# Softmax row sums folded once per four slots instead of once per two, values four slots behind, output copies on ScalarE

## The chip, the cores and the metric

The kernel runs on one core of one Trainium2 chip. The metric is device time in microseconds (us). Executions of one kernel agree within about 0.3%, periods between start times inside the traces to about 0.01 us.

## The reference, cut to what matters

There are two independent attention blocks, A and B, of 16 batches, 32 query positions, 32 query heads over 4 key/value heads, 512 keys and head size 128, all in bf16.

```python
q = (x @ wq).reshape(B, Sq, Hq, Dh).transpose(0, 2, 1, 3)
k = repeat(k_cache, 8, axis=1);  v = repeat(v_cache, 8, axis=1)
scores = einsum("bhqd,bhkd->bhqk", q, k) * Dh ** -0.5
o = einsum("bhqk,bhkd->bhqd", softmax(scores), v)
out = o.transpose(0, 2, 1, 3).reshape(B, Sq, Hq * Dh) @ wo     # A and B side by side
```

## The kernel before

The main loop has 128 **slots**; a slot is one batch and one key/value head (8 query heads, 256 query columns). In each slot TensorE computes transposed scores into `s_ps` (four matmuls of 256 columns), ScalarE takes the exponential into `p_sb`, VectorE reduces `p_sb` over query position blocks into `parts`, and TensorE multiplies an *earlier* slot's `p_sb` with the values into `ob`, a bank of PSUM (the memory that this program's matmuls write) (four matmuls of 256 columns). Between them, `run(units, n)` issues matmuls of 512 columns from a **stream** of unrelated work: query projections first, output projections (`f_ps`) in the later part. So TensorE has something to do while the softmax chain runs. The **lag** is the number of slots by which the values matmuls run behind the scores: three in this kernel.

The row sums are spread over the partitions. `parts` becomes `cs` ("chunk sums") on VectorE; a small matmul, the **fold**, adds the four quadrants of partitions (the program types `cs` and the fold's matrix float32r; the trace shows them as f32 or fp32r); then VectorE takes the reciprocals, spreads them over columns with a transpose (`r`), and multiplies `ob` with `r` into `oT` ("normalize"). There is only one `ob` bank, and it holds a pair of slots.

```python
def fold_sums(j):                            # j: pair of slots
    cs = pair[j]
    sums = pair[j] = psum.tile([P, 2 * REP], FP32, name="sums", tag="sums", bufs=1)
    nc.tensor.matmul(sums[:], lhsT=fold[:]..., rhs=cs[:]..., start=True, stop=True)

def reciprocals(j):
    nc.vector.reciprocal(out=rall[:, j, :], in_=pair.pop(j)[:])
    r = rcp[j] = work.tile([P, 2 * REP, SQ], FP32, name="r")
    nc.vector.transpose(out=r[:]..., in_=rall[:, j, :].unsqueeze(2).to_broadcast(...))

# at the end of each output tile of the stream (f_units):
    if eng is nc.scalar: nc.scalar.copy(out=o_sb[:, 0:width], in_=ps[:, 0:width])
    else:                nc.vector.tensor_copy(out=o_sb[:, 0:width], in_=ps[:, 0:width])

for i in range(total_slots + 3):
    live = i < total_slots
    j, odd = divmod(i, 2)
    if live:
        do_loads(i); scores(i)
    run(units, 1)
    if not odd and 1 <= j <= NG: chunk_sums(j - 1)
    if i >= 3:                   values(i - 3)
    if odd and 1 <= j <= NG:     reciprocals(j - 1)
    if not odd and j >= 2:       normalize(j - 2)
    run(units, 5)
    if not odd and 1 <= j <= NG: fold_sums(j - 1)
    if live:                     partial_sums(i)
    run(units, 1 - (i % 4 == 3))
```

Of the kernel before, what the change touches and what calls it, by code (L numbers as in the profile page):

```python
# [8 lines left out]
BF16 = mybir.dt.bfloat16  # L9
FP32 = mybir.dt.float32  # L10
FP32R = mybir.dt.float32r
# [5 lines left out]
P = 128  # L17
# [3 lines left out]
REP = HQ // HKV  # L21
# [152 lines left out]
def kernel(  # L174
# [14 lines left out]
    nc = tc.nc  # L189
    B, SQ, D = A_x.shape  # L190
# [3 lines left out]
    KC = SK // P  # L194
    TT = NTOK // P
    NOUT = D
    NW = 512
    NH = NOUT // NW
    GRP = 4
    NG = B * HKV  # L200
    BPT = P // SQ
    QW = REP * SQ
# [7 lines left out]
    def fast_path(ok_i):  # L210
        with ExitStack() as fctx:
            enter = fctx.enter_context
            const = enter(tc.tile_pool(name="const", bufs=1))
            blk = enter(tc.tile_pool(name="blk", bufs=20))
            kv = enter(tc.tile_pool(name="kv", bufs=3))
            work = enter(tc.tile_pool(name="work", bufs=2))
            outp = enter(tc.tile_pool(name="outp", bufs=3))
            psum = enter(tc.tile_pool(name="psum", bufs=2, space=bass.MemoryType.PSUM))
            enter(tc.manual_schedule())

# [5 lines left out]
            nc.scalar.preload_act_table_set("natural_log_exp_and_others")  # L226


            warm = const.tile([P, NW], BF16, name="warm")
            nc.vector.memset(warm[:], 0.0)  # L230
            ident = const.tile([P, P], BF16, name="ident")
            make_identity(nc, ident[:])
# [1 line left out]
            for r in range(P // QD):  # L234
                rs = slice(r * QD, (r + 1) * QD)
                nc.vector.tensor_copy(
                    out=fold[rs],
                    in_=ident[rs, rs].unsqueeze(1).to_broadcast([QD, P // QD, QD]),
# [4 lines left out]
            nc.vector.memset(shift[:], SHIFT)  # L243
            cnt = const.tile([P, 1], FP32, name="cnt")
            nc.vector.memset(cnt[:], 0.0)
            rall = const.tile([P, NG, 2 * REP], FP32, name="rall")


            def blk_tile(shape, name, dtype=BF16):
# [76 lines left out]
            def f_units(pr, tt, n0, width, eng):  # L326
                ps = psum.tile([P, NW], FP32, name="f_ps", tag="proj")
                nh, off = divmod(n0, NW)
                for h in range(HQ):
                    assert all((pr, b, h // REP) in normalized for b in range(tt * BPT, (tt + 1) * BPT))  # L330
                    nc.tensor.matmul(  # L331
                        ps[:, 0:width],
                        lhsT=oT[pr, tt][:, h, :],
                        rhs=wo_tiles[pr, nh, h // REP][:, h % REP, off:off + width],
                        start=(h == 0),
                        stop=(h == HQ - 1),
                    )
                    if h == HQ - 1:
                        o_sb = outp.tile([P, NW], BF16, name="o_sb")
                        if eng is nc.scalar:  # L340
                            nc.scalar.copy(out=o_sb[:, 0:width], in_=ps[:, 0:width])  # L341
                        else:
                            nc.vector.tensor_copy(out=o_sb[:, 0:width], in_=ps[:, 0:width])  # L343
                        c0 = problems[pr][5] + n0
                        eng.dma_start(  # L345
                            out=out_flat[tt * P:(tt + 1) * P, c0:c0 + width],
                            in_=o_sb[:, 0:width],
                        )
                    yield
# [16 lines left out]
            def scores(i):  # L366
                pr, b, g = where(i)
                kT = k_tiles[i // GRP].rearrange("p q (k c) -> p q c k", c=KC)
                s_ps = psum.tile([P, KC, QW], FP32, name="s_ps", tag="s")
                for c in range(KC):  # L370
                    nc.tensor.matmul(  # L371
                        s_ps[:, c, :],
                        lhsT=kT[:, i % GRP, c, :],
                        rhs=qT[pr, g][:, b, :, :].rearrange("p h s -> p (h s)"),
                        start=True,
                        stop=True,
                    )
                p_sb = work.tile([P, KC, QW], BF16, name="p_sb", bufs=5)
                nc.scalar.activation(  # L379
                    out=p_sb[:], in_=s_ps[:], func=ACTF.Exp, bias=shift[:], scale=SCALE  # L380
                )
                st[i] = {"p": p_sb}

            parts, rcp, pair = {}, {}, {}

            def partial_sums(i):
                j, q = divmod(i, 2)
                if q == 0:
                    parts[j] = work.tile([P, 2, KC, REP], FP32, name="parts")
                nc.vector.tensor_reduce(  # L390
                    out=parts[j][:, q, :, :].rearrange("p c h -> p (c h)"),
                    in_=st[i]["p"][:].rearrange("p c (h s) -> p (c h) s", s=SQ),
                    axis=AX.X, op=ALU.add, apply_transpose=True,
                )

            def chunk_sums(j):
                cs = pair[j] = work.tile([P, 2, REP], FP32R, name="cs")
                with nc.allow_low_precision(reason="float32r holds the float32 sum"):
                    nc.vector.tensor_reduce(  # L399
                        out=cs[:], in_=parts.pop(j)[:].rearrange("p q c h -> p q h c"),  # L400
                        axis=AX.X, op=ALU.add,
                    )

            def fold_sums(j):
                cs = pair[j]
                sums = pair[j] = psum.tile([P, 2 * REP], FP32, name="sums", tag="sums", bufs=1)
                nc.tensor.matmul(  # L407
                    sums[:],
                    lhsT=fold[:].rearrange("p r s -> p (r s)"),
                    rhs=cs[:].rearrange("p q h -> p (q h)"),  # L410
                    start=True,
                    stop=True,
                )

            def reciprocals(j):
                nc.vector.reciprocal(out=rall[:, j, :], in_=pair.pop(j)[:])  # L416
                r = rcp[j] = work.tile([P, 2 * REP, SQ], FP32, name="r")
                nc.vector.transpose(  # L418
                    out=r[:].rearrange("p n s -> p (n s)"),
                    in_=rall[:, j, :].unsqueeze(2).to_broadcast([P, 2 * REP, SQ]),  # L420
                )

            ob = {}
# [1 line left out]
            def values(i):  # L425
                v_sb = v_tiles[i // GRP]
                j, q = divmod(i, 2)
                if q == 0:
                    ob[j] = psum.tile([P, 2, QW], FP32, name="ob", tag="ob", bufs=1)
                for c in range(KC):  # L430
                    nc.tensor.matmul(  # L431
                        ob[j][:, q, :],
                        lhsT=v_sb[:, i % GRP, c, :],
                        rhs=st[i]["p"][:, c, :],
                        start=(c == 0),
                        stop=(c == KC - 1),
                    )

            def normalize(j):
                for i in (2 * j, 2 * j + 1):  # L440
                    normalized.add(where(i))
                    st.pop(i)
                pr, b, g = where(2 * j)
                tt, bl = divmod(b, BPT)
                if (pr, tt) not in oT:
                    oT[pr, tt] = blk_tile([P, HQ, P], "oT")
                if pr == 0:
                    out = oT[pr, tt][:, g * REP:(g + 1) * REP, bl * SQ:(bl + 2) * SQ]
                    out = out.rearrange("p h (q s) -> p q h s", s=SQ)
                else:  # L450
                    out = oT[pr, tt][:, g * REP:(g + 2) * REP, bl * SQ:(bl + 1) * SQ]
                    out = out.rearrange("p (q h) s -> p q h s", h=REP)
                nc.vector.tensor_tensor(  # L453
                    out=out,
                    in0=rcp.pop(j)[:].rearrange("p (q h) s -> p q h s", h=REP),
                    in1=ob.pop(j)[:].rearrange("p q (h s) -> p q h s", s=SQ),
                    op=ALU.mult,
                )
# [79 lines left out]
            for h, copy in enumerate((nc.vector.tensor_copy, nc.scalar.copy)):  # L538
                copy(
                    out=qT[0, 0][:, :, h, :],  # L540
# [48 lines left out]


            total_slots = 2 * NG
            for i in range(total_slots + 3):
                live = i < total_slots
                j, odd = divmod(i, 2)
                if live:
                    do_loads(i)
                    scores(i)
                run(units, 1)
                if not odd and 1 <= j <= NG:
                    chunk_sums(j - 1)  # L600
                if i >= 3:
                    values(i - 3)
                if odd and 1 <= j <= NG:
                    reciprocals(j - 1)
                if not odd and j >= 2:
                    normalize(j - 2)
                run(units, 5)
                if not odd and 1 <= j <= NG:
                    fold_sums(j - 1)
                if live:  # L610
                    partial_sums(i)
                run(units, 1 - (i % 4 == 3))
# [56 lines left out]
```

## Time and profile before

The time is 350.51 us (median of 4 runs, 349.77 to 350.71); the profiled span is 348.6 us. These are the engine line of the page and some of its groups. PE is TensorE, PEld its weight loads, DVE VectorE, ACT ScalarE and POOL GpSimd; L407 is line 407 of the kernel. In a group line, the numbers after the first bar are total busy us and the mean ns of one instruction; those after the second are the engine's idle us just before them and what ended it.

```profile
PE 342.2 (98%) x2217; PEld 221.2 (63%) x2217; DVE 282.6 (81%) x420; ACT 180.4 (52%) x197; POOL 8.9 (3%) x21
...
L407 PE MATMUL sums<-cs,fold 128*128 128x16 f32 x64 | 22.9, 357 | 0.1
L407 PEld LDWEIGHTS sums<-cs,fold 128*128 128x128 f32 x64 | 12.1, 190 | 8.3 <-DVE cs L399 0.9
L343 DVE CAST o_sb<-f_ps 128x512 bf16<-128x512 f32 (+1 forms) x16 | 10.8, 673 | 10.8 <-PE f_ps L331 10.0
L399 DVE TENSOR_REDUCE cs<-parts 128x16 fp32r<-128x64 f32 x64 | 16.8, 262 | 2.2
L416 DVE RECIPROCAL rall<-sums 128x16 f32<-128x16 f32 x64 | 14.1, 220 | 0.0
```

TensorE is full. The first trap is the line of the folds: 64 of 357 ns look like 22.9 us, but matmuls are pipelined and their ends are modelled, so a mean duration is not what an instruction costs the stream. What it costs must be read from the **starts** of its neighbours. This is the timeline of PE (start us, us, engine, line, operation):

```profile
203.45 1.46 PE L331 MATMUL f_ps<-wo_sb,oT 128*128 128x512 bf16 x6
204.74 0.60 PE L371 MATMUL s_ps<-qT,kT 128*128 128x256 bf16 x4
...
205.83 1.24 PE L331 MATMUL f_ps<-wo_sb,oT 128*128 128x512 bf16 x5
206.72 0.36 PE L407 MATMUL sums<-cs,fold 128*128 128x16 f32 x1
206.94 0.39 PE L331 MATMUL f_ps<-wo_sb,oT 128*128 128x512 bf16 x1
207.17 0.60 PE L371 MATMUL s_ps<-qT,kT 128*128 128x256 bf16 x4
...
209.34 0.60 PE L371 MATMUL s_ps<-qT,kT 128*128 128x256 bf16 x4
...
210.43 1.24 PE L331 MATMUL f_ps<-wo_sb,oT 128*128 128x512 bf16 x5
211.74 0.28 PE L407 MATMUL sums<-cs,fold 128*128 128x16 f32 x1
...
212.10 0.60 PE L371 MATMUL s_ps<-qT,kT 128*128 128x256 bf16 x4
```

Six stream matmuls alone take 204.74 - 203.45 = 1.29 us; six with a fold among them take 207.17 - 205.83 = 1.34 us. So a fold costs about 0.05 us as this view rounds, not 0.357. The score lines work as a clock: from one `s_ps` line to the next is one slot, 2.43 us with a fold (204.74 to 207.17), and 2.385 or 2.17 us for slots of 7 or 6 stream matmuls without, which puts a fold at about 0.045 us. A group of four slots takes 9.407 us, and this repeats through the run.

The slot from 209.34 lasts 2.76 us, 0.33 us too long: the fold starts at 211.74 instead of about 211.3. VectorE's timeline for that stretch shows why:

```profile
209.54 0.69 DVE L343 CAST o_sb<-f_ps 128x512 bf16<-128x512 f32 x1 [0.77 <-PE f_ps L331]
210.15 1.23 DVE L390 TRANSPOSE_TENSOR_REDUCE parts<-p_sb 128x32 f32<-128x1024 bf16 x1
211.41 0.27 DVE L399 TENSOR_REDUCE cs<-parts 128x16 fp32r<-128x64 f32 x1
```

VectorE waited 0.77 us for the stream's output tile, copied it for 0.69 us, and only then came to the partial sums and the chunk sums that the fold needs. There is one other such hole, of about 0.12 us, in the slot from 299.14 us. Together the holes are 0.45 us.

### The profile page before, as it was taken

Reading aid. Unit: us, or ns where it says so; the run is one execution under the profiler, and the core shown is the slowest. Engines: PE = TensorE matmul, PEld = TensorE weight load, DVE = VectorE, ACT = ScalarE, POOL = GpSimd, SP = SyncE. Lnnn points to the kernel's source line nnn. Section 1 sums busy time; section 2 is a strip of 40 time slices with the busy share of each in tenths; the row PEclk is TensorE's granted clock in tenths of the full one; section 3 lists DMA queues with packets and bytes.
Section 4 is the critical chain, followed back from the end, with each engine's and each line's share of the span. In section 5 each row is a group of like instructions: output and inputs, shape, how many; then the busy total and the mean of one; then the engine's idle time right before and its main releaser. Section 6 shows DMA issues by size and latency. Waiting matters only on the chain.

```text
span 348.6 us, 5527 instructions
## 1 busy us (share of the span) xinstructions
PE 342.2 (98%) x2217; PEld 221.2 (63%) x2217; DVE 282.6 (81%) x420; ACT 180.4 (52%) x197; POOL 8.9 (3%) x21
## 2 busy tenths in 40 slices
PE   7999999999999999999999999999999999999995
PEld 4556666666666666666666666666666666666554
DVE  2118988888988889898889989999999999899710
ACT  3347667666666766666654454454455445445000
POOL 0000000000000000000000000000000000000010
PEclk9999999999999999999999999999999999999999
DMA  7999999899997899999999459995589995400000
GB/s 224 240 302 333 168 253 270 241 276 256 270 253 197 172 249 222 311 267 268 279 316 222 115 124 270 349 212 121 137 259 263 252 227 102 120 18 0 15 32 20
DMA packets 125069, 71.70 MB, mean 206 GB/s; under 512 B 73616, under 2 KB 124048, under 8 KB 125040
## 3 DMA queue, kind: packets, MB, share of 16 engines
q1 hardware_dynamic: 124176, 69.29, 81.7%
q0 software_dynamic: 720, 1.97, 1.7%
q8 instruction: 18, 0.29, 0.3%
q14 instruction: 11, 0.09, 0.1%
q10 hardware_dynamic: 144, 0.07, 0.1%
HBM read 51.38 MB, written 2.10 MB: 153 GB/s over the span
## 4 chain that ended last, share of the span: by engine, by line
PE 96%; DMA 2%; SPq 1%; DVE 1%; issue 0%; ACT 0%
PE f_ps L331 32%; PE q_ps L312 31%; PE ob L431 16%; PE s_ps L371 16%; DMA x_sb<-in_A_x_dram 2%; PE q_ps L516 1%; SPq L468 0%; DVE parts L390 0%; PE sums L407 0%; SPq L471 0%; DVE o_sb L343 0%; PE xT_ps L506 0%; ACT o_sb L341 0%; DVE cs L399 0%; PE ok_ps L627 0%
## 5 line engine op out<-in xcount | busy, mean ns | idle before, releaser
L379 ACT ACTIVATE p_sb<-s_ps,shift 128x1024 bf16<-128x1024 f32 x128 | 142.5, 1113 | 113.1 <-PE s_ps L371 100.4
L390 DVE TRANSPOSE_TENSOR_REDUCE parts<-p_sb 128x32 f32<-128x1024 bf16 x128 | 158.2, 1236 | 22.1 <-ACT p_sb L379 21.6
L331 PE MATMUL f_ps<-wo_sb,oT 128*128 128x512 bf16 (+1 forms) x544 | 133.3, 367 | 0.0
L312 PE MATMUL q_ps<-xT,wq_sb 128*128 128x512 bf16 x496 | 129.6, 380 | 0.0
L371 PE MATMUL s_ps<-qT,kT 128*128 128x256 bf16 x512 | 76.8, 273 | 0.0
L431 PE MATMUL ob<-p_sb,v_sb 128*128 128x256 bf16 x512 | 76.8, 273 | 0.0
L331 PEld LDWEIGHTS <-oT 128*128 128x128 bf16 x544 | 53.0, 98 | 33.8
L312 PEld LDWEIGHTS <-wq_sb 128*128 128x128 bf16 x496 | 48.4, 98 | 34.7 <-DMA wq_sb<-in_A_wq_dram 0.3
L371 PEld LDWEIGHTS <-kT 128*128 128x128 bf16 x512 | 56.9, 113 | 20.9
L431 PEld LDWEIGHTS <-v_sb 128*128 128x128 bf16 x512 | 50.1, 98 | 19.8 <-DVE oT L453 0.2
L453 DVE TENSOR_TENSOR oT<-r,ob 128x512 bf16<-128x512 f32 x64 | 43.9, 685 | 12.8 <-PE ob L431 9.4
L418 DVE STREAM_TRANSPOSE r<-rall 128x512 f32<-128x512 f32 x64 | 45.5, 711 | 2.2
L320 ACT CAST qT<-q_ps 128x512 bf16<-128x512 f32 x62 | 36.1, 583 | 21.3 <-PE q_ps L312 19.2
L407 PE MATMUL sums<-cs,fold 128*128 128x16 f32 x64 | 22.9, 357 | 0.1
L343 DVE CAST o_sb<-f_ps 128x512 bf16<-128x512 f32 (+1 forms) x16 | 10.8, 673 | 10.8 <-PE f_ps L331 10.0
L399 DVE TENSOR_REDUCE cs<-parts 128x16 fp32r<-128x64 f32 x64 | 16.8, 262 | 2.2
L407 PEld LDWEIGHTS sums<-cs,fold 128*128 128x128 f32 x64 | 12.1, 190 | 8.3 <-DVE cs L399 0.9
L345 POOL DMA_DIRECT2D out_dram<-o_sb x15 | 8.2, 549 | 329.3 <-DVE o_sb L343 298.6
L416 DVE RECIPROCAL rall<-sums 128x16 f32<-128x16 f32 x64 | 14.1, 220 | 0.0
L341 ACT CAST o_sb<-f_ps 128x256 bf16<-128x256 f32 x1 | 0.4, 372 | 22.1 <-PE f_ps L331 22.1
L509 DVE COPY xT<-xT_ps 128x512 bf16<-128x512 bf16 x4 | 1.7, 424 | 5.6 <-PE xT_ps L506 5.6
L509 ACT COPY xT<-xT_ps 128x512 bf16<-128x512 bf16 x4 | 2.3, 585 | 5.7 <-PE xT_ps L506 5.7
(27 smaller groups left out, 24.1 us busy)
## 6 DMA issues: line engine op xcount, KB each, us to landing
v_sb<-in_A_v_cache_dram SPq DMA_DIRECT2D x16, 512.0 KB, 5.0
wq_sb<-in_B_wq_dram SPq DMA_DIRECT2D x8, 1024.0 KB, 6.5
wo_sb<-in_A_wo_dram SPq DMA_DIRECT2D x8, 1024.0 KB, 7.6
v_sb<-in_B_v_cache_dram SPq DMA_DIRECT2D x16, 512.0 KB, 4.5
wo_sb<-in_B_wo_dram SPq DMA_DIRECT2D x8, 1024.0 KB, 8.8
wq_sb<-in_A_wq_dram SPq DMA_DIRECT2D x7, 1024.0 KB, 7.4
out_dram<-o_sb POOLq DMA_DIRECT2D x15, 128.0 KB, 3.6
x_sb<-in_A_x_dram SPq DMA_DIRECT2D x4, 256.0 KB, 3.9
```

What stands on the lines that cost most here:

```text
L312: nc.tensor.matmul(ps[:], lhsT=w[:, dc, (h % 4) * DH:(h % 4 + 1) * DH], rhs=xT[pr][:, dc, :], start=(dc == 0), stop=(dc == DC - 1),)
L320: nc.scalar.copy(out=qT[pr, g][:, :, hl, :], in_=ps[:].rearrange("p (b s) -> p b s", s=SQ),)
L331: nc.tensor.matmul(ps[:, 0:width], lhsT=oT[pr, tt][:, h, :], rhs=wo_tiles[pr, nh, h // REP][:, h % REP, off:off + width], start=(h == 0), ...
L371: nc.tensor.matmul(s_ps[:, c, :], lhsT=kT[:, i % GRP, c, :], rhs=qT[pr, g][:, b, :, :].rearrange("p h s -> p (h s)"), start=True, stop=True,)
L379: nc.scalar.activation(out=p_sb[:], in_=s_ps[:], func=ACTF.Exp, bias=shift[:], scale=SCALE)
L390: nc.vector.tensor_reduce(out=parts[j][:, q, :, :].rearrange("p c h -> p (c h)"), in_=st[i]["p"][:].rearrange("p c (h s) -> p (c h) s", s=SQ),
L399: nc.vector.tensor_reduce(out=cs[:], in_=parts.pop(j)[:].rearrange("p q c h -> p q h c"), axis=AX.X, op=ALU.add,)
L407: nc.tensor.matmul(sums[:], lhsT=fold[:].rearrange("p r s -> p (r s)"), rhs=cs[:].rearrange("p q h -> p (q h)"), start=True, stop=True,)
L416: nc.vector.reciprocal(out=rall[:, j, :], in_=pair.pop(j)[:])
L418: nc.vector.transpose(out=r[:].rearrange("p n s -> p (n s)"), in_=rall[:, j, :].unsqueeze(2).to_broadcast([P, 2 * REP, SQ]),)
L431: nc.tensor.matmul(ob[j][:, q, :], lhsT=v_sb[:, i % GRP, c, :], rhs=st[i]["p"][:, c, :], start=(c == 0), stop=(c == KC - 1),)
L453: nc.vector.tensor_tensor(out=out, in0=rcp.pop(j)[:].rearrange("p (q h) s -> p q h s", h=REP), in1=ob.pop(j)[:].rearrange("p q (h s) -> p ...
```

## The change

`k` now counts groups of four slots, and `o`, from 0 to 3, is a slot's place in its group. The intent: half as many folds on TensorE, fewer small operations and no output copies on VectorE. `chunk_sums`, `fold_sums` and `reciprocals` work on four slots; the spread is a function of its own for each pair; values run four slots behind, because the first pair's reciprocals now come only with the second pair's. The space comes from one output buffer and from `warm`.

```diff
-            outp = enter(tc.tile_pool(name="outp", bufs=3))
+            outp = enter(tc.tile_pool(name="outp", bufs=2))
-            warm = const.tile([P, NW], BF16, name="warm")
+            warm = work.tile([P, NW], BF16, name="warm", tag="p_sb", bufs=6)
-            rall = const.tile([P, NG, 2 * REP], FP32, name="rall")
+            rall = const.tile([P, NG // 2, GRP * REP], FP32, name="rall")
...
-                        if eng is nc.scalar:
-                            nc.scalar.copy(out=o_sb[:, 0:width], in_=ps[:, 0:width])
-                        else:
-                            nc.vector.tensor_copy(out=o_sb[:, 0:width], in_=ps[:, 0:width])
+                        nc.scalar.copy(out=o_sb[:, 0:width], in_=ps[:, 0:width])
...
-                p_sb = work.tile([P, KC, QW], BF16, name="p_sb", bufs=5)
+                p_sb = work.tile([P, KC, QW], BF16, name="p_sb", bufs=6)
...
-                sums = pair[j] = psum.tile([P, 2 * REP], FP32, name="sums", tag="sums", bufs=1)
+                sums = quad[k] = psum.tile([P, GRP * REP], FP32, name="sums", tag="sums", bufs=1)
...  (chunk_sums, reciprocals likewise; the transpose moves to spread(j))
-            for i in range(total_slots + 3):
+            LAG = GRP
+            for i in range(total_slots + LAG):
                 live = i < total_slots
-                j, odd = divmod(i, 2)
+                k, o = divmod(i, GRP)
+                j, odd = divmod(i - LAG, 2)
+                folds = k >= 1 and k <= total_slots // GRP
...
-                if not odd and 1 <= j <= NG:
-                    chunk_sums(j - 1)
-                if i >= 3:
-                    values(i - 3)
-                if odd and 1 <= j <= NG:
-                    reciprocals(j - 1)
-                if not odd and j >= 2:
-                    normalize(j - 2)
+                if o == 0 and folds:
+                    chunk_sums(k - 1)
+                if i >= LAG:
+                    values(i - LAG)
+                if o == 1 and folds:
+                    reciprocals(k - 1)
+                    spread(2 * k - 2)
+                if o == 3 and folds:
+                    spread(2 * k - 1)
+                if odd and j >= 0:
+                    normalize(j)
                 run(units, 5)
-                if not odd and 1 <= j <= NG:
-                    fold_sums(j - 1)
+                if o == 0 and folds:
+                    fold_sums(k - 1)
...
```

More of the change, by code (lines that the diff above doesn't have):

```diff
@@ L382, in scores @@
                 st[i] = {"p": p_sb}
-            parts, rcp, pair = {}, {}, {}
+            parts, rcp, quad = {}, {}, {}
             def partial_sums(i):
-                j, q = divmod(i, 2)
+                k, q = divmod(i, GRP)
                 if q == 0:
-                    parts[j] = work.tile([P, 2, KC, REP], FP32, name="parts")
+                    parts[k] = work.tile([P, GRP, KC, REP], FP32, name="parts", bufs=1)
                 nc.vector.tensor_reduce(
-                    out=parts[j][:, q, :, :].rearrange("p c h -> p (c h)"),
+                    out=parts[k][:, q, :, :].rearrange("p c h -> p (c h)"),
                     in_=st[i]["p"][:].rearrange("p c (h s) -> p (c h) s", s=SQ),
@@ L394, in partial_sums, with chunk_sums, fold_sums @@
                 )
-            def chunk_sums(j):
-                cs = pair[j] = work.tile([P, 2, REP], FP32R, name="cs")
+            def chunk_sums(k):
+                cs = quad[k] = work.tile([P, GRP, REP], FP32R, name="cs", bufs=1)
                 with nc.allow_low_precision(reason="float32r holds the float32 sum"):
                     nc.vector.tensor_reduce(
-                        out=cs[:], in_=parts.pop(j)[:].rearrange("p q c h -> p q h c"),
+                        out=cs[:], in_=parts.pop(k)[:].rearrange("p q c h -> p q h c"),
                         axis=AX.X, op=ALU.add,
                     )
-            def fold_sums(j):
-                cs = pair[j]
-                sums = pair[j] = psum.tile([P, 2 * REP], FP32, name="sums", tag="sums", bufs=1)
+            def fold_sums(k):
+                cs = quad[k]
+                sums = quad[k] = psum.tile([P, GRP * REP], FP32, name="sums", tag="sums", bufs=1)
                 nc.tensor.matmul(
@@ L413, in fold_sums, with reciprocals, spread @@
                 )
-            def reciprocals(j):
-                nc.vector.reciprocal(out=rall[:, j, :], in_=pair.pop(j)[:])
+            def reciprocals(k):
+                nc.vector.reciprocal(out=rall[:, k, :], in_=quad.pop(k)[:])
+            def spread(j):
+                k, o = divmod(j, 2)
                 r = rcp[j] = work.tile([P, 2 * REP, SQ], FP32, name="r")
@@ L419, in reciprocals @@
                     out=r[:].rearrange("p n s -> p (n s)"),
-                    in_=rall[:, j, :].unsqueeze(2).to_broadcast([P, 2 * REP, SQ]),
+                    in_=rall[:, k, o * 2 * REP:(o + 1) * 2 * REP]
+                    .unsqueeze(2).to_broadcast([P, 2 * REP, SQ]),
                 )
```

## The prediction

> **What bounds the kernel now.** TensorE. Page part 1: PE 98% of 348.6 us, DVE 81%, ACT 52%; granted clock 1.000. In the timeline of PE five 128x512 matmuls start in 1.08 us, 0.216 us each, without holes. The Trainium skill, "TensorE: Matmul & The Clock Gate", section "Wait — 56ns, not 53.3ns?", gives N ÷ 2.4 GHz plus about 2.5 ns, 215.7 ns; the trace agrees. The chain of waits is 96% PE.
>
> The score matmuls give a slot clock: 2.43 us for an even slot (7 stream matmuls, 8 of 256 columns, one fold), 2.385 us for a 7-matmul odd slot without fold, 2.17 us for a 6-matmul odd slot; 9.41 us per four slots. Only two groups of four are longer, by 0.33 us near 210 us (the fold waits for chunk sums, behind a VectorE queue made late by an output copy) and 0.11 us near 299 us. So this change can touch 64 folds at 0.045 us (2.43 less 2.385), 2.9 us, plus 0.45 us of holes.
>
> **What changes.**
> - PE: 32 folds of 32 columns replace 64 of 16. I estimate 0.045 to 0.07 us each: 0.6 to 1.4 us saved, about 1.1, all on the critical path. That section's floor of about 25 ns for small matmuls suggests mostly fixed cost; 0.045 is more, perhaps the weight load's (190 ns against 98).
> - VectorE: per four slots, two chunk sums (0.262) and two reciprocals (0.220) become one each, somewhat longer: about 0.35 us less. The 16 output copies (10.8 us) leave. Its load in the output phase falls from about 9.3 to 8.3 of 9.4 us: off the critical path, except for the 0.45 us of holes, which should go.
> - ScalarE: gains 16 copies at about 0.58 (its 512-column copy out of PSUM), 9 us, where it is half busy. Free.
> - Lag 4 instead of 3: one slot with values moves from start to tail; no net PE work.
>
> **New waits that I checked.** VectorE becomes uneven: slots with o=1 carry reciprocal 0.23, spread 0.71, normalize 0.69, partial sums 1.24 = 2.87 us in a 2.39 us slot; o=3 carries 2.64 in 2.17; even ones 1.24 to 1.6. The single `ob` bank must be normalized before the next slot's values: I work out the normalize's end 2.4 us after slot start against a need at 3.04 (o=1), 2.1 against 2.8 (o=3); late exponentials cut this to about 0.35 us. The fold wants its chunk sums at 2.17 us; they end at about 1.55. So no stall, with less slack. Two output buffers suffice: a buffer is reused after 7 us or more, against 3.6 us to landing. The tail's last normalize ends about 0.3 us before its first reader.
>
> **Prediction.** 350.49 - 1.1 - 0.45 + 0.25 (small new holes) = 349.2 us; range 348.0 to 350.7. Chances: faster by over 2% 0.02, within 2% 0.94, slower by over 2% 0.04.
>
> **What the profile would show.** Right: four-slot period 9.36 to 9.39 us; no longer groups; 32 folds; VectorE down about 14 us, ScalarE up about 9; chain over 95% PE. Wrong: values matmuls waiting for `oT` (normalize), folds for `cs`, a period above 9.41.
>
> **What would make it wrong.** A slack eaten: partial sums late because exponentials are late, so that `ob` or the fold waits in each group (0.2 us per group would be 6 us, the slower case); a 32-column fold costing twice a 16-column one (no gain); a load delayed by another order of buffer reuse.

## The result, and the profile after

The time is 348.54 us (median of 4 runs, 348.49 to 349.25), against 350.51 us. The ratio is 0.9954, with a 95% interval of 0.9939 to 0.9968. Ratios here are the mean time of one kernel's fast runs over that of the other's of the same rounds, so they are not quite the ratio of the quoted medians. All outputs are right. The gain of 0.5% is clear of the noise; a second, separate measurement is among the experiments below.

The same parts of the page after the change, the engine line and the groups that answer to those of before:

```profile
PE 341.1 (98%) x2185; PEld 218.4 (63%) x2185; DVE 265.8 (77%) x340; ACT 188.9 (54%) x213; POOL 8.9 (3%) x21
...
L340 ACT CAST o_sb<-f_ps 128x512 bf16<-128x512 f32 (+1 forms) x17 | 9.5, 558 | 23.2 <-PE f_ps L331 15.2
...
L396 DVE TENSOR_REDUCE cs<-parts 128x32 fp32r<-128x128 f32 x32 | 12.1, 377 | 1.1
L404 PE MATMUL sums<-cs,fold 128*128 128x32 f32 x32 | 11.7, 367 | 0.0
L413 DVE RECIPROCAL rall<-sums 128x32 f32<-128x32 f32 x32 | 10.3, 320 | 0.5 <-PE sums L404 0.5
```

There are half as many folds and the copies have moved. PE's share is still 98%: this share could not have told one kernel from the other. The timeline of PE can:

```profile
200.96 0.60 PE L368 MATMUL s_ps<-qT,kT 128*128 128x256 bf16 x4
...
203.34 0.60 PE L368 MATMUL s_ps<-qT,kT 128*128 128x256 bf16 x4
...
203.99 0.60 PE L432 MATMUL ob<-p_sb,v_sb 128*128 128x256 bf16 x4
...
205.72 0.60 PE L368 MATMUL s_ps<-qT,kT 128*128 128x256 bf16 x4
...
207.89 0.60 PE L368 MATMUL s_ps<-qT,kT 128*128 128x256 bf16 x4
...
208.54 0.60 PE L432 MATMUL ob<-p_sb,v_sb 128*128 128x256 bf16 x4
...
209.87 0.37 PE L404 MATMUL sums<-cs,fold 128*128 128x32 f32 x1
...
210.32 0.60 PE L368 MATMUL s_ps<-qT,kT 128*128 128x256 bf16 x4
```

The four slots from 200.96 to 210.32 (o=1, 2, 3 and then 0) take 9.36 us. Only the last of them (207.89 to 210.32) has a fold, and that slot takes 2.43 us, as before, although the fold is twice as wide. No group in the run is longer. VectorE in the same stretch:

```profile
201.48 0.32 DVE L413 RECIPROCAL rall<-sums 128x32 f32<-128x32 f32 x1
201.84 0.71 DVE L418 STREAM_TRANSPOSE r<-rall 128x512 f32<-128x512 f32 x1
202.65 0.69 DVE L454 TENSOR_TENSOR oT<-r,ob 128x512 bf16<-128x512 f32 x1
...
207.07 0.69 DVE L454 TENSOR_TENSOR oT<-r,ob 128x512 bf16<-128x512 f32 x1
...
208.94 0.38 DVE L396 TENSOR_REDUCE cs<-parts 128x32 fp32r<-128x128 f32 x1
```

This is the slack account: the first normalize (L454) ends at 203.34 and the next values matmuls, which need its `ob` bank, start at 203.99, 0.65 us later. The second ends at 207.76 against 208.54. The chunk sums end at 209.32 and their fold starts at 209.87. Everything arrives in time.

**Where the time came from.** Two fewer folds in every eight slots, 32 in all, at 0.043 us (derived below) are 1.39 us; the two holes are 0.45 us. That makes 1.84 us of the 1.9 us between the profiled spans (348.6 and 346.7). The rest is the start: the first scores begin at 22.41 instead of 22.56 us, which varies from run to run. The lag moves one slot's values matmuls from the start of the loop to its end: 0.44 us less before slot 4 and 0.46 us more after the last scores, close to nothing in sum.

### The profile page after: what moved, and what is told of

Same layout as the page of the kernel before. It is cut to its first block, busy times and chain, and to the rows that moved or that the text cites. A ratio compares the mean times of both kernels' runs of the same rounds, so it can differ in the third digit from the quotient of the medians.

```text
span 346.7 us, 5462 instructions
## 1 busy us (share of the span) xinstructions
PE 341.1 (98%) x2185; PEld 218.4 (63%) x2185; DVE 265.8 (77%) x340; ACT 188.9 (54%) x213; POOL 8.9 (3%) x21
## 4 chain that ended last, share of the span: by engine, by line
PE 98%; ACT 0%; issue 0%; DVE 0%; DVEq 0%; ACTq 0%
PE f_ps L331 32%; PE q_ps L312 31%; PE s_ps L368 16%; PE ob L432 16%; PE q_ps L517 1%; PE warm_ps L492 1%; PE xT_ps L507 1%; PE sums L404 0%; ACT o_sb L340 0%; DVE warm L230 0%; PE ok_ps L634 0%; DVEq L671 0%; ACTq L340 0%
## 5 line engine op out<-in xcount | busy, mean ns | idle before, releaser
L454 DVE TENSOR_TENSOR oT<-r,ob 128x512 bf16<-128x512 f32 x64 | 44.0, 687 | 8.8 <-PE ob L432 2.3
L418 DVE STREAM_TRANSPOSE r<-rall 128x512 f32<-128x512 f32 x64 | 44.2, 691 | 1.1
L340 ACT CAST o_sb<-f_ps 128x512 bf16<-128x512 f32 (+1 forms) x17 | 9.5, 558 | 23.2 <-PE f_ps L331 15.2
L396 DVE TENSOR_REDUCE cs<-parts 128x32 fp32r<-128x128 f32 x32 | 12.1, 377 | 1.1
L404 PE MATMUL sums<-cs,fold 128*128 128x32 f32 x32 | 11.7, 367 | 0.0
L413 DVE RECIPROCAL rall<-sums 128x32 f32<-128x32 f32 x32 | 10.3, 320 | 0.5 <-PE sums L404 0.5
L404 PEld LDWEIGHTS sums<-cs,fold 128*128 128x128 f32 x32 | 6.1, 190 | 3.8
L492 PE MATMUL warm_ps<-warm 128*128 128x512 bf16 x7 | 3.4, 630 | 1.3 <-DVE warm L230 1.3
```

Source lines behind the costliest of these rows:

```text
L396: nc.vector.tensor_reduce(out=cs[:], in_=parts.pop(k)[:].rearrange("p q c h -> p q h c"), axis=AX.X, op=ALU.add,)
L404: nc.tensor.matmul(sums[:], lhsT=fold[:].rearrange("p r s -> p (r s)"), rhs=cs[:].rearrange("p q h -> p (q h)"), start=True, stop=True,)
L413: nc.vector.reciprocal(out=rall[:, k, :], in_=quad.pop(k)[:])
L418: nc.vector.transpose(out=r[:].rearrange("p n s -> p (n s)"), in_=rall[:, k, o * 2 * REP:(o + 1) * 2 * REP] .unsqueeze(2).to_broadcast([P, ...
L454: nc.vector.tensor_tensor(out=out, in0=rcp.pop(j)[:].rearrange("p (q h) s -> p q h s", h=REP), in1=ob.pop(j)[:].rearrange("p q (h s) -> p ...
```

## The experiments

The theory is that the gain has two separate terms, a fixed cost for each fold on TensorE, and holes that VectorE's output copies caused. The rivals are that VectorE's lower load gave the gain (its mean load matters), or that the longer lag did. Group times below are the mean of 30 groups of four slots, from the start of slot 4's scores to that of slot 124's, divided by 30, without holes; holes are what the traces have beyond that up to the last slot's scores.

| kernel | folds | lag | copies on | group us | holes us | time us (median) | ratio (95%) |
|---|---|---|---|---|---|---|---|
| before | 64 x 16 columns | 3 | VectorE | 9.407 | 0.45 | 350.51 | 1 |
| copies_only | 64 x 16 | 3 | ScalarE | 9.407 | 0 | 350.12 | 0.9987 (0.9974 to 1.0) |
| lag_only | 64 x 16 | 4 | VectorE | 9.407 | 1.5 | 352.07 | 1.0039 (1.0024 to 1.0054) |
| lag_copies | 64 x 16 | 4 | ScalarE | 9.407 | 0 | 350.50, one run | |
| folds_only | 32 x 32 | 4 | VectorE | 9.363 | 2.3 | 351.31 | 1.0027 (1.0012 to 1.0042) |
| the change | 32 x 32 | 4 | ScalarE | 9.363 | 0 | 348.54 | 0.9954 (0.9939 to 0.9968) |

Each ratio is taken against the kernel before in the same rounds (median 350.49 us in those of the first experiments, 350.56 us in the later ones).

The traces also allow a check without the rounds. From the first scores to the end of the span, which leaves the varying start out, copies_only, lag_copies and fold_again (described below), the kernels with 64 folds and no holes, took 325.68 us each. With 32 folds and no holes, the change, its repetition change_again and spare_o2 took 324.28 to 324.29 us. That is 1.40 us for 32 folds, 0.044 us each.

### Parts of the change alone

**copies_only**: the kernel before with the copies moved.

```diff
-                        if eng is nc.scalar: ... else: nc.vector.tensor_copy(...)
+                        nc.scalar.copy(out=o_sb[:, 0:width], in_=ps[:, 0:width])
```

> Only the copies move to ScalarE; pairs are still folded 64 times with values three slots behind. Theory (the gain is two separate terms: about 0.045 us per fold saved on TensorE, plus 0.44 us of holes that VectorE's copies caused): the 0.33 us and 0.11 us holes go, the four-slot period stays 9.41 us, the time is about 0.45 us below the kernel before (ratio about 0.9987). Rival (VectorE's load is what gave the whole gain): a period nearer 9.36 us and about 1.5 to 2 us gained (ratio about 0.995).

As the theory said: both holes are gone, the group stays at 9.407 us. The ratio is 0.9987, whose interval just touches 1; the holes are the firmer evidence. The profile's VectorE share fell from 81% to 79% and groups without a hole did not move, which speaks against VectorE's load as such; the runs with a spare operation, below, test it directly.

**folds_only**: the changed kernel with the copies put back on VectorE.

```diff
-                        nc.scalar.copy(out=o_sb[:, 0:width], in_=ps[:, 0:width])
+                        if eng is nc.scalar: ... else: nc.vector.tensor_copy(...)
```

> Folds over four slots and values four slots behind, but the output copies stay on VectorE. Theory: the period is 9.36 us in all groups without a hole, and 1.4 us is gained there; but the odd slots now carry up to 2.9 us of VectorE work, so some of the 16 copies of 0.67 us that fall in them push the normalize past the next values: I expect new holes of 0.1 to 0.5 us each, 0.3 to 1.5 us in all, in the output phase only, and a ratio of 0.996 to 1.000. Rival (the copies do not matter): as the change, ratio about 0.995, no hole.

The group is 9.363 us as expected, so the folds gave what they should. But the holes were larger than I expected, 2.3 us against 0.3 to 1.5, and the stretch after the last scores is 0.4 us longer as well. The result is *slower than the kernel before*. These are the lines of one hole, VectorE and then PE:

```profile
208.43 0.69 DVE L343 CAST o_sb<-f_ps 128x512 bf16<-128x512 f32 x1 [0.34 <-PE f_ps L331]
209.04 1.24 DVE L390 TRANSPOSE_TENSOR_REDUCE parts<-p_sb 128x32 f32<-128x1024 bf16 x1
210.31 0.38 DVE L399 TENSOR_REDUCE cs<-parts 128x32 fp32r<-128x128 f32 x1
```

```profile
209.32 1.24 PE L331 MATMUL f_ps<-wo_sb,oT 128*128 128x512 bf16 x5
210.74 0.28 PE L407 MATMUL sums<-cs,fold 128*128 128x32 f32 x1 [0.18 <-DVE cs L399]
```

It is the same chain as in the hole of the kernel before: the copy waits for the stream and delays partial sums, chunk sums and then the fold, and the stream matmul that the program puts after the fold started only after it (324.75 after 324.61 in the last fold, for one).

This is not the chain that I had expected, which was a late normalize. Of the six holes three are of the kind shown (0.45, 0.34 and 0.17 us). In two (0.35 and 0.36 us) the values did wait for the normalize, and the longest, 0.60 us, has both waits. The 0.4 us at the end is again a fold: from five stream matmuls before the last fold to the next values took 2.00 us (323.19 to 325.19), against 1.56 us in the changed kernel (320.90 to 322.46). A values wait and that last fold:

```profile
223.86 0.60 PE L435 MATMUL ob<-p_sb,v_sb 128*128 128x256 bf16 x4 [0.19 <-DVE oT L457]
...
324.61 0.28 PE L407 MATMUL sums<-cs,fold 128*128 128x32 f32 x1 [0.18 <-DVE cs L399]
```

This run contains the lag of four too, so the holes are those of lag and folds together; the next run has the lag alone.

**lag_only**: the kernel before, with values one slot later (and the memory changes that go with it).

```diff
-            for i in range(total_slots + 3):
+            for i in range(total_slots + 4):
-                if i >= 3:
-                    values(i - 3)
+                if i >= 4:
+                    values(i - 4)
-                if not odd and j >= 2:
+                if odd and j >= 2:
                     normalize(j - 2)
```

> Pairs are still folded 64 times and the copies stay on VectorE; only the values run four slots behind, with six p_sb buffers and two output buffers. Theory: the lag itself is worth nothing: period 9.41 us, holes of 0 to 1 us in the output phase, ratio 0.999 to 1.002. Rival (the longer lag gives the values matmuls room and is the source of the gain): period below 9.40 us, ratio below 0.997.

The lag brings no gain, and it costs more than I expected: holes of 1.5 us instead of 0.45, and the same 0.4 us at the end, at the last fold. The lag moves the normalize from the even slots, where it came after the chunk sums, to the odd slots, ahead of the partial sums that the next chunk sums need. So a copy that falls there can delay a fold more often. The weight loads of the folds waited for `cs` (total us, times, longest) 2 times in the kernel before, the first line, and 9 times here, the second:

```profile
PEld sums L407 <- DVE cs L399: 0.9, 2, 0.6
PEld sums L407 <- DVE cs L399: 3.0, 9, 0.6
```

In two slots the values waited for the normalize as well (0.1 and 0.3 us). That there is one output buffer less is not the cause: none of VectorE's waits in this trace is for a transfer.

**lag_copies**: the same with the copies on ScalarE (the two edits above together).

> Pairs folded 64 times, values four slots behind, and the output copies on ScalarE. Theory (the lag puts the normalize behind more VectorE work in odd slots, so that it cannot bear VectorE's copies, and the copies' move repays exactly that): the holes of 1.5 us and the late tail of the run with the lag alone vanish, period 9.41 us throughout, time as in the run with the copies alone, about 350.1 us. Rival (the lag costs something else, such as the tail slot): 350.8 us or more.

All holes are gone, at 9.407 us for a group. The single time, 350.50 us, lies between my two numbers and decides nothing: this run's first scores began at 23.02 us, 0.46 us later than in the trace of before, and from the last scores to the end it took 28.6 us, as in the changed kernel. From the first scores to the end it took 325.68 us, as copies_only did. So the lag costs nothing once VectorE's copies are gone.

**lag3**: the changed kernel with values only three slots behind. The first pair of a quad must then be normalized before the values in the slot with o=1.

```diff
-            LAG = GRP
+            LAG = 3
+                if o == 1 and folds:
+                    reciprocals(k - 1); spread(2 * k - 2); normalize(2 * k - 2)
                 if i >= LAG:
                     values(i - LAG)
-                if o == 1 and folds: ... spread(2 * k - 2)   # and o == 3, and normalize(j)
+                if o == 2 and folds:
+                    spread(2 * k - 1); normalize(2 * k - 1)
```

> Four-slot folds with the values still three slots behind: the first pair of a quad can be normalized only after the reciprocals, so in slots with o=1 the values matmuls wait in order for reciprocal, spread and normalize. From the changed kernel's trace the normalize ends about 2.4 us after the start of that slot and the values would start at 0.65 us: a hole of 1.2 to 1.9 us in every group, period 10.5 to 11.3 us, 385 to 412 us in all. Rival (the lag of four is not needed): period 9.36 to 9.5 us.

It took 404.29 us, and a group 11.09 us: a hole of 1.73 us in every slot with o=1, as expected. The wait of PE (total us, times, longest) names it:

```profile
PE ob L432 <- DVE oT L454: 50.6, 32, 1.8
```

With one `ob` bank and this order of work, folding by four pays only with the lag of four.

### What a fold costs

**fold_again**: the changed kernel, with each fold issued a second time two slots later.

```diff
+                if o == 2 and folds:
+                    fold_again(k - 1)      # the same matmul into the same sums tile, already read
```

> The changed kernel, with each 32-column fold issued a second time, to no purpose, two slots later: 64 folds of 32 columns, VectorE as in the changed kernel. Theory (a fold costs TensorE about 0.045 us whatever its width up to 32): period back to 9.41 us, time 1.4 us above the changed kernel, about 0.5 us below the kernel before (ratio about 0.9985). Rival (the fold is free and VectorE's saved operations gave the gain): period 9.36 us, ratio about 0.995.

The group went back to 9.407 us: 0.0434 us for each extra fold. The ratio to the kernel before was 0.9981 (0.9968 to 0.9994). VectorE's work was that of the changed kernel (265.8 us busy in both), so the rival that folds are free falls. It also settles the width: without any fold a group would take 9.363 - 0.0434 = 9.320 us, and the kernel before, with two folds of 16 columns, takes 9.407 = 9.320 + 2 x 0.0434. So 16 and 32 columns cost the same.

**fold_wide**: the same 32 sums repeated to 128 columns.

```diff
-                    rhs=cs[:].rearrange("p q h -> p (q h)"),
+                    rhs=cs[:].rearrange("p q h -> p (q h)").unsqueeze(1).to_broadcast([P, 4, GRP * REP]),
...  (the sums tile is four times as wide; the reciprocals read its first quarter)
```

> The changed kernel, with each fold made four times as wide: the same 32 sums repeated to 128 columns by the access pattern. Read from the slot clock of the trace. If a fold's cost is fixed up to some width (theory: the float32 weight load or the issue sets it, 0.045 us), the fold slot grows from 2.43 us to at most 2.46 us; if the columns stream at a rate that counts already at 32 columns (rival), it grows by 0.04 us or more: 0.04 us for 96 more columns at the rate of the bf16 matmuls (0.216 us for 512), 0.16 us if float32 needs four passes.

The group took 9.396 us, so a fold of 128 columns costs 9.396 - 9.320 = 0.076 us, 0.032 us more for 96 more columns. Columns do count somewhere between 32 and 128, at most at the rate of the bf16 stream (96 columns at 0.216 us for 512 would be 0.040 us). Four passes, 0.16 us (4 x 0.040), are ruled out for this float32r matmul. By its slot of 2.46 us it sits on the border that I had set; the equal cost of 16 and 32 columns decides for a fixed cost there.

**fold_bf16** and **fold_bf16_timed**: the fold matrix and `cs` in bf16, first one look, then timed.

```diff
-            fold = const.tile([P, P // QD, QD], FP32R, name="fold")
+            fold = const.tile([P, P // QD, QD], BF16, name="fold")
-                cs = quad[k] = work.tile([P, GRP, REP], FP32R, name="cs", bufs=1)
+                cs = quad[k] = work.tile([P, GRP, REP], BF16, name="cs", bufs=1)
```

> The changed kernel, with the fold matrix and the chunk sums in bf16, so that the fold's weight load takes about 98 ns instead of 190 ns. If the 0.045 us per fold comes from the longer float32 weight load (my guess in the prediction), the fold slot shrinks from 2.43 us to about 2.41 us or less (cost 0.025 us or less); if not, it stays 2.42 to 2.43 us. The result stays within tolerance, being a sum of 128 terms rounded to bf16 each.

The weight load and the matmul of the bf16 fold, in fold_bf16_timed's listing of the tile `fold` (duration in ns: minimum, median, maximum):

```profile
L404 PEld LDWEIGHTS <-fold x32: 97/98/98, 31.4 to 320.7; 128*128 128x128 bf16 x32
L404 PE MATMUL sums<-cs,fold x32: 179/179/180, 31.6 to 320.9; 128*128 128x32 bf16 x32
```

The group took 9.346 us: a bf16 fold costs 0.026 us, 0.017 us less than the float32r one. So about two fifths of the fold's cost come with the float32r type, whose weight load takes 190 ns instead of 98 ns. The matmul changed type as well, so that the weight load alone does it is likely, not shown. The remaining 0.026 us is close to the floor of about 25 ns start-to-start for small matmuls that the Trainium skill gives ("TensorE: Matmul & The Clock Gate", section "Wait — 56ns, not 53.3ns?").

> The bf16 fold, timed. Its trace showed a group of four slots 0.017 us shorter than in the changed kernel, 32 groups: 0.5 us faster than the changed kernel if it holds in the time (ratio to the kernel before about 0.993 to 0.995), at the price of sums that are rounded to bf16 before they are folded. Rival (the single time of 348.23 us was chance): the same as the changed kernel within 0.2 us.

> The changed kernel itself once more, beside the next run on the same chip: ratio 0.994 to 0.9965, period 9.363 us.

In the same rounds the changed kernel took 348.91 us, ratio 0.9953 (0.9936 to 0.997), confirming the result; the bf16 fold took 347.89 us, ratio 0.9931 (0.9916 to 0.9946). The medians of the two differ by 1.0 us, more than the 0.55 us of 32 x 0.017; part of the rest is a start that was 0.32 us earlier in the profiled run (21.90 against 22.22). The intervals overlap, so the times alone do not separate the two; the slot clock does, and so does the stretch from the first scores to the end, 323.75 and 323.78 us in the two bf16 traces against 324.29 us in change_again. It is the best version that I ran, correct within the test's tolerance, at the price of sums rounded to bf16 before the fold.

### Is it VectorE's load or its order?

**spare_o1** and **spare_o2**: the changed kernel, with one useless extra spread per group, in the slots with o=1 or in those with o=2.

```diff
 # spare_o1
                     spread(2 * k - 2)
+                    spread(2 * k - 2)
 # spare_o2
+                if o == 2 and folds:
+                    spread(2 * k - 1)
...  (in both, the second call writes the same tile again)
```

> The changed kernel, with the reciprocal spread (0.70 us of VectorE) done twice, the second time to no purpose, in the slots with o=1. The slack account says that the normalize ends 2.38 us after the slot's start and is needed at 3.03 us: with 0.70 us more it ends at 3.08 us plus a semaphore, so that the first values matmul of the next slot waits 0.1 to 0.25 us in every group of four: period 9.46 to 9.6 us, 3 to 8 us in all. Rival (only the mean load of VectorE counts, 77% before and about 84% after): period stays 9.36 us.

> The same extra spread of 0.70 us, once per four slots, but in the slots with o=2, where VectorE sits idle about 0.63 us before the partial sums. Same total VectorE work as the run with o=1. Slack account: partial sums start about 0.1 to 0.2 us later, nothing on TensorE waits, period stays 9.36 us, time within 0.2 us of the changed kernel. Rival (mean load counts): the same loss as with o=1.

The engine line of the page of spare_o1, and then that of spare_o2:

```profile
PE 345.1 (98%) x2185; PEld 217.4 (62%) x2185; DVE 285.1 (81%) x372; ACT 189.1 (54%) x213; POOL 8.9 (3%) x21
```

```profile
PE 340.6 (98%) x2185; PEld 218.1 (63%) x2185; DVE 284.9 (82%) x372; ACT 188.9 (54%) x213; POOL 8.9 (3%) x21
```

VectorE did the same work, 285 us. With o=2 the group stayed at 9.363 us (348.74 us, one run). With o=1 it grew to 9.510 us, by 0.147 us, and the run took 354.06 us. VectorE and then PE of spare_o1, in a group whose slot with o=1 starts at 213.52:

```profile
214.44 1.46 DVE L420 STREAM_TRANSPOSE r<-rall 128x512 f32<-128x512 f32 x2
216.01 0.69 DVE L456 TENSOR_TENSOR oT<-r,ob 128x512 bf16<-128x512 f32 x1
```

```profile
216.34 0.38 PE L331 MATMUL f_ps<-wo_sb,oT 128*128 128x512 bf16 x1
216.75 0.60 PE L434 MATMUL ob<-p_sb,v_sb 128*128 128x256 bf16 x4
```

The normalize ends at 216.70 and the values start at 216.75. After one stream matmul they would have started 0.216 us after 216.34, at about 216.56, so they waited. The slack of 0.65 us read from the changed kernel is therefore real: 0.7 us more uses it up. And the same load in another place cost nothing, so VectorE's mean load is not what counts here.

## Why the prediction was right or wrong

The prediction was right: 349.2 us, range 348.0 to 350.7, against 348.54 us measured. The range also holds 350.51 us, no change at all, so lying in it says little. The sharper forecast was the period, 9.36 to 9.39 us with no longer groups, and it was met at 9.363 us. The terms:

- **The folds** were estimated at 0.045 to 0.07 us each, for a gain of "about 1.1" us. They cost 0.0434 us at either width, so the gain was 1.39 us, the upper end of my 0.6 to 1.4. The fear that 32 columns might cost twice 16 was wrong. The guess that the float32 weight load is part of it is supported by the bf16 run, for about 0.017 us of the 0.043.
- **The holes** of 0.45 us went, as predicted, and the copies on ScalarE were free. But I called the copies' move a gain of 0.45 us; its real part is larger. Without it, four-slot folding with its lag had 2.3 us of holes and was slower than before. I had not worked out the change without it.
- **"Small new holes", 0.25 us**: there were none. This and the folds are most of the miss: 350.49 (from which the prediction started) - 1.39 - 0.45 = 348.65 us, 0.1 us from the measured median.
- **The slack account** held. I predicted the normalize's end at 2.4 us and the need at 3.04 us after the start of a slot with o=1; the trace has 2.38 and 3.03. For o=3 it was 2.1 and 2.8, and is 2.04 and 2.82. For the fold, chunk sums at 1.55 and need at 2.17 are 1.43 and 1.98. In the tail I gave about 0.3 us, which was far too little. The last normalize ends at 327.68 us. The stream matmuls after the last values begin at 326.79 us, and the seventh of them, at about 328.08, opens the last block of rows; but it reads head 0, which an earlier pair had filled. By the kernel's loops the last pair fills heads 16 to 31, and the first matmul to read those is the 23rd, at about 331.76 us, 4.1 us after the normalize.
- **Sizes off, without effect**: the reciprocal of 32 columns takes 0.320 us, not 0.23, and the chunk sums 0.377 us, so VectorE saves 0.27 us per group instead of 0.35. "VectorE down about 14 us" did not even follow from my own numbers (32 x 0.35 + 10.8 = 22 us); the page shows 16.8 us less busy time. ScalarE rose by 8.5 us, against about 9.

## What to carry to other kernels

On a saturated engine, price an instruction by what it adds between the starts of its neighbours, and compare two kernels by a period inside the traces: here 0.043 us per group was plain there, while starts alone varied by 1.1 us between runs. On an engine that feeds it, mean load says little: what counts is when each result ends and when it is needed, and an instruction that must wait for the saturated engine (here an output copy) is a bad thing to put in front of such a result. Parts of a change need not add up: here the folds by four with their lag, tried without moving the copies, would have been rejected as slower.

## What the Trainium skill lacked or had wrong

- "TensorE: Matmul & The Clock Gate", section "Wait — 56ns, not 53.3ns?": the floor of about 25 ns for small matmuls agrees with the bf16 fold among full-size matmuls (0.026 us), but nothing is said of float32r, where the same fold costs 0.043 us. The same page's section "Weight-path perf modes — Fast Weight Load (FWL) and DoubleRow" says that the fast weight load (FWL) is off for FP32 and does not name float32r; if that counts as FP32 there, weight loads of 190 ns against 98 ns agree.
- "FP8 and Floating Point Precision", section "TensorE Precision Notes", gives four passes for true FP32 and no cost for float32r: here 96 more float32r columns cost 0.032 us, so it is not four passes.
- "VectorE: DVE Perf Modes", section "First, the fixed hardware budget", says that reciprocal repeats its divide 8 times, but gives no time: 16 more columns cost 0.100 us (0.220 to 0.320 us), 6.3 ns a column.
- "Perfetto Trace Analysis", section "Identifying the Most-Contended Engine", calls occupancy a fair measure of how close VectorE is to its limit. Here two runs with 285 us of VectorE work each differed by 4.7 us in their groups (32 x 0.147): for an engine that feeds another, the page lacks the slack of each result.
- No page gives the spread, from run to run, of the time before a kernel's main loop: the first scores began between 21.90 and 23.02 us in the traces of these kernels, though the code before them is nearly the same.
